# Cached attention and MLP over two layers: kept heads' scores in pairs, the first P.V of layer two ahead of the next scores, next queries under the maximum, last w4 rows apart

## The chip, the cores and the metric

One core of one Trainium2 chip. The metric is the device time of one execution in microseconds (us). A run of the kernel before and one of the kernel after are compared on the same chip; smaller is faster.

## What is computed

One token passes two layers, and each layer is an attention over a cached window and a small MLP. Both layers use the same weights and the same cache. Cut to what matters:

```python
# D = 640, 32 heads of Dh = 192, window W = 4096 of 32768 positions, F = 1536
def A(x):                                   # x: one row of 640
    q = (x @ wq).reshape(32, 192)
    s = einsum("hd,hkd->hk", q, k_cache[:, -4096:]) * 192 ** -0.5
    o = einsum("hk,hkd->hd", softmax(s), v_cache[:, -4096:])
    return o.reshape(6144) @ wo
def B(x):
    x1 = x + shifts(gelu(ln(x) @ w1)) @ w2  # the shifts move one row out: zero for S = 1
    return x1 + gelu(ln(x1) @ w3) @ w4
for _ in range(2):
    x = x + A(ln(x))
    x = x + B(ln(x))
```

With a sequence of one row every shifted part of the first MLP is zero, so w1 and w2 are never loaded. What remains to be loaded is 218 MB: for each layer 32 heads of keys and of values at 1536 KB each, wo, w3 and w4; wq once.

## The kernel before, in words

**Groups and slots.** The 32 heads form eight groups of four (`G`). One buffer ("slot") holds 128 x 6144 bf16, that is 12,288 bytes in each partition or 1536 KB: the keys of one head, its values, its transposed keys, or a fifth of wq. There are 15 slots; five hold wq for the whole run. A list `free` hands them out: `slot()` takes the one at the front, and a slot is put back at the end when the program has no further use of it. The order of `free` is fixed when the program is built, so the slot that a load will go to, and with it the instruction that the load waits for, is set by the order in which the program is written. One more buffer, `half` (128 x 3072), holds by turns the exponentials E and their transpose ET, the probabilities PT, the blocks of queries (`Q8_two`), and at the end of a layer the last rows of w4.

**Loads.** SyncE issues all loads in one queue, strictly in order. The list comes from `plan`: first the keys of the first group, then for each group its values alternating with the keys of the next group, and wo; at the end w3 and w4 (`load_w34`, L136 to L149). Each issue waits until the last reader of its slot is done, and for the load eight before it (eight semaphores are used in turn). `ahead` and `need` advance through the list.

**One head's scores.** The keys lie in HBM with positions along partitions; VectorE transposes them in 32 x 32 blocks in two halves (`trans_begin`, `trans_end`, L324; 1.75 us each) into a free slot. `kmm` (L350, products on L364) then multiplies a block of queries with the transposed keys: 12 products of 512 columns, whose outputs are 8 rows each. An output's first row chooses a column tile of TensorE's array: head 0 and 2 of a group use the tiles at rows 0 and 32, heads 1 and 3 those at rows 64 and 96. All products of a group go to one PSUM tile, `S_ps`.

**Queries.** `qproj` (L296) makes the queries of a group: 30 products with wq (`qT_ps`, L301), a spread by VectorE (`Xq`, L305), one product (`Qrep_ps`, L309), and a masked block by VectorE (L312). `qpair_a` and `qpair_b` (L272 to L294) do the same for two heads at a time.

**Softmax.** `soft_a` (L378) takes the maximum of each row (L380), transposes it on TensorE (L384) and takes the maximum again (L386). `soft_b` brings it back (L392) and takes the exponentials on ScalarE (L396). `soft_c` transposes them on VectorE (L402), moves them into place with 16 small products (L411) and copies the result to PT on ScalarE (L417); between these it ends the half transposed keys of the next group's first head.

**P.V.** `pv_rows` (L462, L471) multiplies a head's probabilities with its values: 16 products of 384 columns on four column tiles. For the last group of a layer the last two heads go through `pv_cols`.

**Order around the change.** Layer one runs the groups 0 to 7, layer two 7 to 0. Layer one leaves the transposed keys and the values of group 7 in eight slots, so layer two begins "warm": `attention` computes the scores of four kept heads at once with `kmm`, one head after the other, with the queries in two halves. Five loads are called for at this point (`need(G + 1)`): into the two slots of w3 and w4, and into the slots of the first three kept heads' transposed keys. Then follow softmax, the first half transpose of the next group's first head, that group's queries, and the rest of the softmax. In the main loop, for each head i, the next group's keys are transposed and multiplied first, and P.V of the current group's head i follows; behind i = 1 the queries of the group after next are made ahead of P.V.

**End of a layer.** `mixer` (L641) is the MLP: 60 products with w3 (L655), GELU, 60 with w4 (L666). The last 20 of these read four row blocks of w4 that one load of 640 KB brings into `half` (L147).

Of the kernel before, what the change touches and what calls it, by code (L numbers as in the profile page):

```python
# [8 lines left out]
BF16 = mybir.dt.bfloat16  # L9
# [15 lines left out]
def kernel(  # L25
# [110 lines left out]
    def load_w34():  # L136
# [11 lines left out]
            half[:, D - P:HALF].rearrange("p (k n) -> p k n", n=D),  # L148
            B_w4[(NB4 + 1) * P:NF * P, :].rearrange("(k p) n -> p k n", p=P))  # L149
# [122 lines left out]
    def qpair_a(g, x, xn_bf):  # L272
        qT_ps = psm.tile([P, NOC // 2], F32, tag="psm", name="qT_ps")
        for tl in range(NOC // 2):
            t = g * NOC + x * (NOC // 2) + tl
            for kc in range(ND):
                nc.tensor.matmul(
                    qT_ps[:, tl:tl + 1], lhsT=wq_t[kc][:, t * P:(t + 1) * P], rhs=xn_bf[:, kc:kc + 1],
                    start=(kc == 0), stop=(kc == ND - 1))
        Xq = sm.tile([P, NOC // 2, 4], BF16, name="Xq")  # L280
        nc.vector.tensor_tensor(
            out=Xq[:], in0=qT_ps[:, :].unsqueeze(2).broadcast_to([P, NOC // 2, 4]),
            in1=maskq[:, :].unsqueeze(1).broadcast_to([P, NOC // 2, 4]), op=ALU.mult)
        return Xq

    def qpair_b(g, x, Xq):
        Qrep_ps = psm.tile([P, 2 * NCOL], F32, tag="psm", name="Qrep_ps")
        nc.tensor.matmul(Qrep_ps[:], lhsT=Lb[:].rearrange("p a i -> p (a i)"), rhs=Xq[:].rearrange("p t b -> p (t b)"), start=True, stop=True)
        if x == 0:
            Q_t[g] = Q8_two[nq[0] % 2]  # L290
            nq[0] += 1
        nc.vector.tensor_tensor(
            out=Q_t[g][:, x], in0=Qrep_ps[:, :].unsqueeze(2).broadcast_to([P, 2 * NCOL, 8]),
            in1=blk8[:, x, :].unsqueeze(1).broadcast_to([P, 2 * NCOL, 8]), op=ALU.mult)  # L294

    def qproj(g, xn_bf):  # L296
        qT_ps = psm.tile([P, NOC], F32, tag="psm", name="qT_ps")
        for tl in range(NOC):
            t = g * NOC + tl
            for kc in range(ND):  # L300
                nc.tensor.matmul(  # L301
                    qT_ps[:, tl:tl + 1], lhsT=wq_t[kc][:, t * P:(t + 1) * P], rhs=xn_bf[:, kc:kc + 1],
                    start=(kc == 0), stop=(kc == ND - 1))
        Xq = sm.tile([P, NOC, 4], BF16, name="Xq")
        nc.vector.tensor_tensor(  # L305
            out=Xq[:], in0=qT_ps[:, :].unsqueeze(2).broadcast_to([P, NOC, 4]),
            in1=maskq[:, :].unsqueeze(1).broadcast_to([P, NOC, 4]), op=ALU.mult)
        Qrep_ps = psm.tile([P, NOC * 4], F32, tag="psm", name="Qrep_ps")
        nc.tensor.matmul(Qrep_ps[:], lhsT=Lb[:].rearrange("p a i -> p (a i)"), rhs=Xq[:].rearrange("p t b -> p (t b)"), start=True, stop=True)  # L309
        Q8 = Q8_two[nq[0] % 2]  # L310
        nq[0] += 1
        nc.vector.tensor_tensor(  # L312
            out=Q8,
            in0=Qrep_ps[:, :].rearrange("p (x c) -> p x c", x=2).unsqueeze(3).broadcast_to([P, 2, 2 * NCOL, 8]),
            in1=blk8[:].unsqueeze(2).broadcast_to([P, 2, 2 * NCOL, 8]), op=ALU.mult)
        Q_t[g] = Q8

# [32 lines left out]
    def kmm(g, i):  # L350
        h = g * G + i
        if i == 0:
            S_t[g] = S_two[nS[0] % 2]
            nS[0] += 1
        S_ps = S_t[g]
        T = T_t[h]
        x, par = i // 2, i % 2
        n = 0
        for f in range(NFB):
            for t in range(2):  # L360
                for hf in range(2):
                    Tv = T[:, hf * HALF:(hf + 1) * HALF].rearrange("p (f c t) -> p f c t", f=NFB, t=2)
                    r = 32 * (2 * par + hf)
                    nc.tensor.matmul(  # L364
                        S_ps[r:r + 8, :], lhsT=Q_t[g][:, x, par * NCOL + 2 * f + t, :], rhs=Tv[:, f, :, t],
                        start=(x == 0 and n == 0), stop=(n == NCOL - 1), tile_position=(0, r),
                        skip_group_check=True)
                n += 1
        if h not in keep_T:
            free.append(T_t.pop(h))  # L370
# [7 lines left out]
    def soft_a(g):  # L378
# [5 lines left out]
        nc.tensor.transpose(pmT_ps[0:G, :], pmh[:, 0:G], ident[:, :])  # L384
        ngm = sm.tile([G, 1], F32, name="ngm")
# [156 lines left out]
    def attention(order, xT_cur, xT_new, keep, loads):  # L542
# [30 lines left out]
        if warm:  # L573
            qpair_b(g0, 0, qpair_a(g0, 0, xn_bf))
            kmm(g0, 0)
            Xq = qpair_a(g0, 1, xn_bf)
            kmm(g0, 1)
            qpair_b(g0, 1, Xq)
            kmm(g0, 2)
            kmm(g0, 3)  # L580
            need(G + 1)
        else:
            qproj(g0, xn_bf)
            for i in range(G):
                keys(g0 * G + i)
                kmm(g0, i)
                if i == 0:
                    qproj(g1, xn_bf)
        soft_a(g0)
        soft_b(g0)  # L590
        if warm:
            keys(g1 * G, whole=False)
            qproj(g1, xn_bf)
        soft_c(g0, g1 * G)
        kept = lambda g, i: ("V", g * G + i) in keep
        for n, g in enumerate(order[:-1]):
            nxt = order[n + 1]
            ahead_h = order[n + 2] * G if n + 2 < len(order) else None
            for i in range(G):
                keys(nxt * G + i)  # L600
                kmm(nxt, i)
# [5 lines left out]
                ahead("V", g * G + i)  # L607
# [131 lines left out]
```

## Time and profile before

| What | Value |
|---|---|
| Median of three runs | 535.39 us (534.71 to 535.95) |
| Profiled execution: its own time | 535.32 us |
| Its span, first to last instruction | 533.5 us |
| TensorE, matmul busy | 314.8 us, 59% |
| VectorE busy | 279.2 us, 52% |
| ScalarE busy | 39.2 us, 7% |
| Moved by DMA | 218.76 MB, mean 410 GB/s |
| Mean granted TensorE clock | 0.678 of full speed |

The page gives for each engine its busy time, then the span in 40 slices of 13.3 us with the busy share in tenths, then the DMA queues. q1 is the queue of SyncE's loads; q8 and q14 fetch instructions. "Granted clock" is the share of TensorE's full clock in a stretch; in this trace it is 0.5 or 1.0 at any moment. In timelines a row gives start, duration, engine, line, operation, output and inputs, partitions and elements, and how many instructions were merged into the row; in brackets stands the idle time before it and what ended it. "SPq" is an issue on SyncE's queue. In the table of stretches the columns are the stretch, its length, busy time of PE (TensorE), PEld (its weight loads), DVE (VectorE), ACT (ScalarE) and POOL, then clock, DMA share and GB/s.

### The profile page before, as it was taken

What the parts mean: (1) busy time and instruction counts of PE and PEld (TensorE: products, weight loads), DVE (VectorE), ACT (ScalarE), POOL (GpSimd) and SP (SyncE); (2) the same over time, 40 slices, a digit from 0 to 9 for tenths busy, and PEclk for the clock granted to TensorE, in tenths of its full rate; (3) what the DMA queues carried; (4) which work ended last, traced back from release to release, by engine and by line L of the source; (5) the groups of instructions that cost most, each with busy time, mean ns of one, the idle gap of its engine ahead of it and who ended that gap; (6) DMA issues with size and microseconds to landing.
All of it is one profiled execution on the core that took longest, in us unless ns stands there. A gap on an engine that the chain in (4) does not pass through costs nothing.

```text
span 533.5 us, 8123 instructions
## 1 busy us (share of the span) xinstructions
PE 314.8 (59%) x3598; PEld 149.1 (28%) x3598; DVE 279.2 (52%) x409; ACT 39.2 (7%) x106; POOL 2.1 (0%) x11
## 2 busy tenths in 40 slices
PE   1154756574655656545585776765655657455685
PEld 0011222231322313213155333332322314122154
DVE  4076675465645457264421377775736447454421
ACT  1001010010100001010013001010101001010012
POOL 1000000000000000000000000000000000000000
PEclk9987677766577665776665777768577655756555
DMA  8999999999999999999999889999999999999995
GB/s 346 427 427 424 424 425 426 427 423 426 423 425 427 422 424 424 426 424 425 422 405 354 343 332 430 425 422 423 424 427 425 424 427 421 426 427 421 421 407 198
DMA packets 26151, 218.76 MB, mean 410 GB/s; under 512 B 2692, under 2 KB 7300, under 8 KB 10116
## 3 DMA queue, kind: packets, MB, share of 16 engines
q1 hardware_dynamic: 26106, 218.25, 98.1%
q8 instruction: 28, 0.46, 0.3%
q14 instruction: 7, 0.06, 0.0%
q10 hardware_dynamic: 10, 0.00, 0.0%
HBM read 218.24 MB, written 0.00 MB: 409 GB/s over the span
## 4 chain that ended last, share of the span: by engine, by line
DMA 75%; DVE 10%; PE 10%; SPq 4%; issue 1%; ACT 0%; DVEq 0%
DMA slot<-in_A_k_cache_dram 41%; DMA slot<-in_A_v_cache_dram 31%; DVE slot L324 7%; PE S_ps L364 6%; DMA half<-in_B_w_dram 3%; SPq L145 2%; DVE pm L380 1%; SPq L146 1%; PE O_ps L471 1%; PE qT_ps L301 0%; SPq L109 0%; DVE half L402 0%; PE pmT_ps L384 0%; PE y2T_ps L666 0%; DVE pmh L382 0%
## 5 line engine op out<-in xcount | busy, mean ns | idle before, releaser
L324 DVE STREAM_TRANSPOSE slot<-slot 128x1536 uint32<-128x1536 uint32 x120 | 206.8, 1756 | 84.0 <-DMA slot<-in_A_k_cache_dram 84.0
L364 PE MATMUL S_ps<-slot,half 128*8 128x512 bf16 x768 | 173.8, 558 | 113.9 <-DVE slot L324 112.1
L364 PEld LDWEIGHTS <-half 128*8 128x8 bf16 x768 | 45.5, 103 | 204.9 <-issue 193.9
L471 PE MATMUL O_ps<-slot,half 128*8 128x384 bf16 x512 | 61.7, 445 | 0.0
L471 PE MATMUL O_ps<-slot,PT 128*8 128x384 bf16 x448 | 47.0, 430 | 0.0
L394 ACT COPY nb_sb<-nb_ps 128x1 f32<-128x1 f32 x16 | 2.5, 159 | 425.2 <-PE nb_ps L392 425.2
L380 DVE TENSOR_REDUCE pm<-S_ps 128x1 f32<-128x512 f32 x16 | 11.1, 692 | 38.7 <-PE S_ps L364 38.7
L305 DVE TENSOR_TENSOR Xq<-qT_ps,maskq 128x24 bf16<-128x24 f32 x15 | 2.7, 179 | 50.3 <-PE qT_ps L301 50.3
L471 PEld LDWEIGHTS <-half 128*8 128x8 bf16 x512 | 19.7, 98 | 19.0 <-issue 16.3
L510 PE MATMUL OX_ps<-half,hoX 128*128 128x192 f32 x26 | 13.1, 608 | 15.6 <-DVE half L504 15.6
L301 PE MATMUL qT_ps<-xn_bf,slot 128*128 128x1 bf16 x450 | 14.2, 164 | 12.7 <-DMA slot<-in_A_wq_dram 11.5
L535 PE MATMUL y_ps<-osb,wo_g 128*128 128x1 bf16 x480 | 15.4, 165 | 10.5 <-DVE osb L516 9.2
L535 PEld LDWEIGHTS <-wo_g 128*128 128x128 bf16 x480 | 16.0, 105 | 16.0 <-issue 15.3
L471 PEld LDWEIGHTS <-PT 128*8 128x8 bf16 x448 | 15.3, 99 | 17.3 <-issue 14.7
L301 PEld LDWEIGHTS <-slot 128*128 128x128 bf16 x450 | 12.8, 97 | 19.8 <-DMA slot<-in_A_wq_dram 13.1
L384 PE MATMUL pmT_ps<-ident,pmh 128*4 128x128 f32 x16 | 5.0, 314 | 18.1 <-DVE pmh L382 18.1
L411 PE MATMUL Pp_ps<-half,identb 128*32 128x32 bf16 x256 | 6.6, 235 | 15.2 <-DVE half L402 15.2
L402 DVE STREAM_TRANSPOSE half<-half 128x512 bf16<-128x512 bf16 x16 | 11.0, 685 | 4.8 <-ACT half L396 4.8
L512 DVE TENSOR_TENSOR half<-OX_ps,m 128x192 f32<-128x192 f32 x13 | 4.7, 358 | 14.3 <-PE OX_ps L510 14.3
L411 PEld LDWEIGHTS <-identb 128*32 128x32 bf16 x256 | 5.8, 115 | 21.5 <-issue 21.1
L510 PEld LDWEIGHTS OX_ps<-half,hoX 128*128 128x128 f32 x26 | 6.5, 312 | 16.7 <-DVE half L504 16.7
L396 ACT ACTIVATE half<-S_ps,nb_sb 128x512 bf16<-128x512 f32 x16 | 11.0, 688 | 0.5
(116 smaller groups left out, 169.5 us busy)
## 6 DMA issues: line engine op xcount, KB each, us to landing
slot<-in_A_k_cache_dram SPq DMA_DIRECT2D x60, 1536.0 KB, 28.1
slot<-in_A_v_cache_dram SPq DMA_DIRECT2D x60, 1536.0 KB, 28.1
wo_g<-in_A_wo_dram SPq DMA_DIRECT2D x14, 960.0 KB, 28.1
slot<-in_A_wq_dram SPq DMA_DIRECT2D x5, 1536.0 KB, 13.2
slot<-in_B_w_dram SPq DMA_DIRECT2D x2, 1536.0 KB, 23.8
slot<-in_B_w_dram SPq DMA_DIRECT2D x2, 1120.0 KB, 19.4
half<-in_B_w_dram SPq DMA_DIRECT2D x2, 640.0 KB, 8.4
slot<-in_B_w_dram SPq DMA_DIRECT2D x2, 384.0 KB, 17.8
```

Source lines behind the costliest of these rows:

```text
L145: nc.sync.dma_start(b[:, FB4:FREE], B_w4[NB4 * P:(NB4 + 1) * P, 0:FREE - FB4])
L146: nc.sync.dma_start(half[:, 0:D - P], B_w4[NB4 * P:(NB4 + 1) * P, P:D])
L301: nc.tensor.matmul(qT_ps[:, tl:tl + 1], lhsT=wq_t[kc][:, t * P:(t + 1) * P], rhs=xn_bf[:, kc:kc + 1], start=(kc == 0), stop=(kc == ND - 1))
L324: nc.vector.transpose(T[:, hf * HALF:(hf + 1) * HALF].bitcast(U32).rearrange("p (f j k) -> p j f k", f=NFB, j=HJ, k=32), Kn[:, hf * HALF:( ...
L364: nc.tensor.matmul(S_ps[r:r + 8, :], lhsT=Q_t[g][:, x, par * NCOL + 2 * f + t, :], rhs=Tv[:, f, :, t], start=(x == 0 and n == 0), stop=(n ...
L380: nc.vector.tensor_reduce(out=pm[:], in_=S_t[g][:], op=ALU.max, axis=AX.X)
L396: nc.scalar.activation(out=E, in_=S_ps[:], func=ACTF.Exp, bias=nb_sb[:, 0:1], scale=scale, accum_out=lpart[:, 0:1])
L402: nc.vector.transpose(ET.rearrange("p (j r) -> p j r", r=32), E.rearrange("p (j k) -> p j k", k=32))
L411: nc.tensor.matmul(two, lhsT=identb[:, 32 * tl:32 * (tl + 1)], rhs=ETv[:, :, 0:2, m].rearrange("p (j e) x -> p x j e", e=2), start=True, s ...
L471: nc.tensor.matmul(O_t[g][r:r + 8, :], lhsT=PT[:, i, jj, :], rhs=V[:, jj * 2 * Dh:(jj + 1) * 2 * Dh], start=(i == 0 and jj < 4), stop=(i = ...
L510: nc.tensor.matmul(OX_ps[:], lhsT=hoX[:].rearrange("p h i -> p (h i)"), rhs=O_sb, start=True, stop=True)
L535: nc.tensor.matmul(y_ps[:, n:n + 1], lhsT=wo_t[g][:, 3 * pr + t, n * P:(n + 1) * P], rhs=osb[:, pr, t:t + 1], start=(first and t == chunks ...
```

## The change

Four edits. (1) The load of the last four row blocks of w4 becomes two: three row blocks, then one. (2) `kmm` takes a list of heads of a pair and interleaves their products; the four kept heads run as two pairs over four column tiles, and the second half of the queries is projected ahead of the first pair. In all other places `kmm` gets one head, as before. (3) The query functions are cut anew into `q_project` (products with wq), `q_spread` (Xq and Qrep) and `q_block`; at the start of layer two the next group's 30 products come ahead of the softmax, and `soft_a` calls `q_spread` behind the transpose of the maximum (`between`); the first half transpose of keys comes after the block of queries and `soft_b`. (4) In the first turn of the main loop of layer two, P.V of head i comes ahead of the next group's transposes and scores of head i. In all other turns the new `values(i)` is called where P.V stood, but the queries of the group after next, at i = 1, now follow it.

```diff
@@ load_w34
-            half[:, D - P:HALF].rearrange("p (k n) -> p k n", n=D),
-            B_w4[(NB4 + 1) * P:NF * P, :].rearrange("(k p) n -> p k n", p=P))
+            half[:, D - P:HALF - D].rearrange("p (k n) -> p k n", n=D),
+            B_w4[(NB4 + 1) * P:(NF - 1) * P, :].rearrange("(k p) n -> p k n", p=P))
+        nc.sync.dma_start(half[:, HALF - D:HALF], B_w4[(NF - 1) * P:NF * P, :])
@@ queries (qpair_a, qpair_b and the body of qproj become)
+    def q_project(g, xn_bf, xs=(0, 1)):
+        n = NOC // 2 * len(xs)
+        qT_ps = psm.tile([P, n], F32, tag="psm", name="qT_ps")
+        for tl in range(n):
+            t = g * NOC + xs[0] * (NOC // 2) + tl
             for kc in range(ND):
                 nc.tensor.matmul(
...
+        return qT_ps
+
+    def q_spread(qT_ps):
+        n = qT_ps.shape[1]
+        Xq = sm.tile([P, n, 4], BF16, name="Xq")
...
+        return Qrep_ps
+
+    def q_block(g, Qrep_ps, xs=(0, 1)):
+        if xs[0] == 0:
             Q_t[g] = Q8_two[nq[0] % 2]
             nq[0] += 1
...
     def qproj(g, xn_bf):
+        q_block(g, q_spread(q_project(g, xn_bf)))
@@ scores
-    def kmm(g, i):
-        h = g * G + i
-        if i == 0:
+    def kmm(g, x, pars):
+        if x == 0 and 0 in pars:
...
         for f in range(NFB):
             for t in range(2):
-                for hf in range(2):
...
+                for par in pars:
+                    T = T_t[g * G + 2 * x + par]
+                    for hf in range(2):
+                        Tv = T[:, hf * HALF:(hf + 1) * HALF].rearrange("p (f c t) -> p f c t", f=NFB, t=2)
+                        r = 32 * (2 * par + hf)
+                        nc.tensor.matmul(
+                            S_ps[r:r + 8, :], lhsT=Q_t[g][:, x, par * NCOL + 2 * f + t, :], rhs=Tv[:, f, :, t],
...
-    def soft_a(g):
+    def soft_a(g, between=None):
...
         nc.tensor.transpose(pmT_ps[0:G, :], pmh[:, 0:G], ident[:, :])
+        if between is not None:
+            between()
@@ attention, start of layer two
         if warm:
-            qpair_b(g0, 0, qpair_a(g0, 0, xn_bf))
-            kmm(g0, 0)
-            Xq = qpair_a(g0, 1, xn_bf)
-            kmm(g0, 1)
-            qpair_b(g0, 1, Xq)
-            kmm(g0, 2)
-            kmm(g0, 3)
+            Qrep_ps = q_spread(q_project(g0, xn_bf, (0,)))
+            q_block(g0, Qrep_ps, (0,))
+            qT_ps = q_project(g0, xn_bf, (1,))
+            kmm(g0, 0, (0, 1))
+            q_block(g0, q_spread(qT_ps), (1,))
+            kmm(g0, 1, (0, 1))
             need(G + 1)
+            qT_ps = q_project(g1, xn_bf)
+            got = []
+            soft_a(g0, lambda: got.append(q_spread(qT_ps)))
+            q_block(g1, got[0])
+            soft_b(g0)
+            keys(g1 * G, whole=False)
...
-        soft_a(g0)
-        soft_b(g0)
-        if warm:
-            keys(g1 * G, whole=False)
-            qproj(g1, xn_bf)
...
         soft_c(g0, g1 * G)
@@ attention, main loop
+            def values(i):
+                ahead("V", g * G + i)
+                if i == 0:
+                    norm_rows(g)
+                pv_rows(g, i, kept(g, i))
+
             for i in range(G):
+                first_v = warm and n == 0
+                if first_v:
+                    values(i)
                 keys(nxt * G + i)
-                kmm(nxt, i)
+                kmm(nxt, i // 2, (i % 2,))
...
-                ahead("V", g * G + i)
+                if not first_v:
+                    values(i)
                 if i == 1 and ahead_h is not None:
                     qproj(order[n + 2], xn_bf)
-                if i == 0:
-                    norm_rows(g)
-                pv_rows(g, i, kept(g, i))
```

## The prediction, made before the change was run

> **What bounds the kernel now.** I read the page's part 2 first (one column of the line is 13.3 us), then its part 3.
>
> ```profile
> DMA  8999999999999999999999889999999999999995
> GB/s 346 427 427 424 424 425 426 427 423 426 423 425 427 422 424 424 426 424 425 422 405 354 343 332 430 425 422 423 424 427 425 424 427 421 426 427 421 421 407 198
> q1 hardware_dynamic: 26106, 218.25, 98.1%
> q8 instruction: 28, 0.46, 0.3%
> ```
>
> The 16 DMA engines move 421 to 430 GB/s nearly always; the compute engines are 59% busy or less. The loads set the time, and only places where the DMA engines run dry can be won: the first column, the last, and four columns around 267 to 320 us, where layer one ends and layer two begins. Next, busy time by stretches of that region:
>
> ```profile
> 296.50:297.50 1.00, 1.00 (x6) 0.13 (x3) 0.00 (x0) 0.00 (x0) 0.00 (x0) 0.50 0.21 86
> 297.50:298.50 1.00, 1.00 (x21) 0.69 (x21) 0.17 (x1) 0.00 (x0) 0.00 (x0) 0.50 0.06 25
> 298.50:299.50 1.00, 1.00 (x12) 0.27 (x8) 0.00 (x0) 0.00 (x0) 0.00 (x0) 0.90 0.72 135
> ...
> 310.00:311.00 1.00, 1.00 (x14) 0.32 (x12) 1.00 (x1) 0.00 (x0) 0.00 (x0) 0.50 0.27 111
> 311.00:312.00 1.00, 1.00 (x16) 0.54 (x12) 1.00 (x2) 0.00 (x0) 0.00 (x0) 0.50 0.06 25
> 312.00:313.00 1.00, 0.75 (x8) 0.21 (x4) 0.86 (x1) 0.00 (x0) 0.00 (x0) 0.83 0.60 111
> 313.00:314.00 1.00, 1.00 (x10) 0.36 (x9) 0.00 (x0) 0.00 (x0) 0.00 (x0) 1.00 0.55 184
> ```
>
> The last two columns are DMA share and GB/s. Against 430 GB/s the first hole lacks 0.80 + 0.94 + 0.69 us and 0.14 in the next us: **2.6 us**. The second lacks 0.74 + 0.94 + 0.74 + 0.57: **3.0 us**. What they wait for is in SyncE's timeline (the issues):
>
> ```profile
> 289.51 0.33 SPq L116 DMA_DIRECT2D slot<-in_A_k_cache_dram  x1
> 297.61 0.33 SPq L116 DMA_DIRECT2D slot<-in_A_k_cache_dram  x1
> 299.85 0.33 SPq L116 DMA_DIRECT2D slot<-in_A_k_cache_dram  x1
> 301.83 0.33 SPq L116 DMA_DIRECT2D slot<-in_A_k_cache_dram  x1
> 311.61 0.33 SPq L116 DMA_DIRECT2D slot<-in_A_v_cache_dram  x1
> 312.72 0.33 SPq L116 DMA_DIRECT2D slot<-in_A_k_cache_dram  x1
> ```
>
> A 1536 KB load takes 3.69 us of DMA. The load of 289.51 is through at about 296.6. The next needs the slot of a kept head's keys, free when that head's scores end at 297.57. Three such loads last until 310.3; the one after them waits for head 0 of the next group (scores end 311.5). First bytes follow an issue by 0.96 us (297.61 to 298.57, 311.61 to 312.57 in the trace's packets).
>
> Last, the end of the chain of waits:
>
> ```profile
> 521.11 8.61 DMA half<-in_B_w_dram
> 529.71 0.05 issue
> 529.76 0.71 PE y2T_ps L666 x20
> 530.49 0.17 DVE x L670
> ```
>
> All 20 last w4 products wait for one 640 KB transfer.
>
> **Part 1: last w4 rows apart (both layers).** Products of one column follow each other by 27 ns (36 in 0.95 us from 288.36). Now 15 of the 20 need only the first three row blocks, so 15 x 0.027 = 0.40 us can run before the last bytes. On the slowest DMA engine the last block is 8 packets of 1280 bytes, 52 ns apart: 0.41 us, just enough to cover them. One more issue on SyncE costs 0.38 us. In layer one the load behind it is not issued until 287.53, 4.9 us later; at the end only the output is behind it, 10 us later. One more semaphore write per engine is 0.009 us. **-0.4 us at the end**, and queries 0.4 us earlier in layer two. Were the two transfers to land together, 0; bounds -0.45 to 0.1.
>
> **Part 2: scores two heads at a time.** The kept heads' scores today and a P.V that uses four column tiles:
>
> ```profile
> 294.85 2.72 PE L364 MATMUL S_ps<-slot,half 128*8 128x512 bf16 x12 [0.35 <-DVE half L292]
> 300.28 1.98 PE L364 MATMUL S_ps<-slot,half 128*8 128x512 bf16 x24 [0.35 <-DVE half L292]
> ```
> ```profile
> 272.00 2.73 PE L471 MATMUL O_ps<-slot,PT 128*8 128x384 bf16 x32
> ```
>
> Head 0: 12 products in 2.72 us at clock 0.5, six steps of two, 0.427 us apart. Heads 2 and 3: 24 in 1.98 us at clock 1.0; where both heads' products are in flight, four start within 20 ns and the next four 0.225 us later. P.V: 32 products in eight steps of four, 0.32 us apart, at clock 0.5. So four tiles step as fast as two, and a pair costs 5 x 0.427 + 0.63 = 2.76 us at clock 0.5 and 5 x 0.225 + 0.39 = 1.5 us at 1.0. The second query projection (15 products, 0.45 us) moves ahead of the pair, but TensorE is idle there from 294.5 to 294.85 for the block of queries: +0.05 us at most. Start 294.85 - 0.40 = 294.45; pair 0 ends at 297.2 (head 0 today: 297.57), Qrep and the block of queries take 0.46 us as today (299.82 to 300.28), pair 1 ends at 299.2 to 300.4, today 302.26. The first hole closes 0.4 us earlier (late DMA engine: 0.1, its last packet ends at 298.45): **-0.3 us**. Its rest stays: nothing frees a slot earlier.
>
> [...] The score row's next weight load starts at 295.24, together with the products of 295.24 and in the 0.63 us of those begun at 294.85, and the steps are 0.427 us, the 512 columns alone. [...]
>
> **Part 3: next queries under the maximum.** Today VectorE does maximum, half a transpose (1.75 us), then Xq, wait for Qrep, block of queries (305.62 to 306.40), then the exponentials' transpose. Now the 30 products (0.90 us) run under the maximum (0.69 + 0.23), Xq and Qrep beside the transpose on TensorE; 0.36 us of VectorE stays ahead of the half transpose. P is ready 5.65 us after the last score instead of 5.86: -0.2 us of a chain that Part 4 takes off the path.
>
> **Part 4: first P.V ahead of the next scores.** P is ready at 299.2..300.4 + 5.65; 16 products take 0.82 us (row at 326.42, clock 1.0) to 1.45 us (four steps of 0.32 and the tail, clock 0.5); V's slot is free at 305.7 to 307.5 and the next load is issued then, not at 311.61. Its first bytes come at 306.7 to 308.5; the loads in flight last until 310.35 - 0.40 = 309.95. So the second hole is gone, with 1.4 to 3.2 us to spare. What is late next: the load behind it in SyncE's order waits for scores of head 0, now behind that P.V: half transpose until 6.4 us after the last score, 2.0 to 3.1 us of scores, so 308.7 to 309.9, needed by 309.95 + 3.69 - 0.96 = 312.7. Then P.V 1, scores 1 (about 312.5, needed by 320) keep ahead. Each us of lateness costs one.
>
> What is the hole worth? For the mean DMA engine 3.0 us. One engine's last packet ends at 312.10 (the next latest 311.18, half by 310.6): a 16 KB instruction packet sat in its row at 307.88 for 1.02 us and doubled the next one to 0.93. It loses only 0.47 us plus 0.6 us of slow first packets, 1.1 us. The end belongs to the latest engine. Bounds 1.1 and 3.0; I take **-2.5 us**, nearer the row of the 16, since one engine had the short gap and the last loads land up to 3.5 us apart anyway.
>
> **Part 5: moved on the way.** From layer one on, the query projection of the group after next follows P.V 1 instead of preceding it. Behind Xq on VectorE queue the transposes of head 2, whose scores free a slot for SyncE. After V 1 lands: P.V 1.45, products 0.9, Xq to queries 0.9, together 3.25 us; head 2's keys land 3.69 us after V 1. Even 1 us late is covered: a load lands 28.1 us after its issue, seven loads deep. **0**; without that cover 1 us in each of 11 groups.
>
> **Sum.** 535.32 (profiled; span 533.5 and 1.8 around it; median of the three runs 535.39) - 0.4 - 0.3 - 2.5 = **532.1 us**.
>
> **Rivals.**
> 1. *Only the late engine counts* (instruction packets pile on one engine): -1.1 - 0.1 - 0.4 gives 533.7. For it: the spread of landings of 3.5 us at the end. Against: at 317.8 us the landings of one load lay within 0.7 us again, and the hits wander. Chance 0.14.
> 2. *The hole stays*, because the first load is freed by P.V but the loads behind it wait on VectorE (two transposes, 3.43 us, per head), and SyncE's queue is in order: only parts 1 and 2 count, 534.6; with noise, no change. Against: the margins above. Chance 0.07.
> 3. *Weight loads lie bare*: 24 x 0.084 us (the load's duration in the score rows) = 2.0 us more for pair 0, so the first hole grows by 1.6 us; second closed: 535.3 + 1.6 - 2.5 - 0.4 = 534.0. Against: steps of 0.427 us. Chance 0.04.
> 4. *Slower: the four tiles run in turn.* Place: pair 0, whose end frees both slots at once. At clock 0.5 24 x 0.427 = 10.2 us, slots free at 304.8, the first hole grows by 7 us; with 3 won elsewhere about 539. It decides from pair 0 over 6.1 us (2.76 + 0.4 + 2.5 + 0.4). For it: no score row at clock 0.5 has four tiles. Against: the four-tile rows above. Chance 0.05.
>
> Forecast 0.70, 531.1 to 533.3 (bounds of its terms, and the runs' scatter of 0.6 us).
>
> **Chances and range.** 0.2% is 1.1 us, about what a measurement of this kernel can tell from none. Faster: 0.70 + 0.13 + 0.02 = 0.85; same: 0.09; slower: 0.06. The range 531.1 to 534.4 takes in the forecast, rivals 1 and 3 and leaves out most of 2 and 4.
>
> **What would show it.** Scores of a pair: 24 products in about 2.8 us; first V load issued by 307.5; DMA share about 1.0 from 300 to 325; a hole of some 2.2 us left around 297; five products after the last transfer. I am wrong if a hole stands after 310, if pair 0 takes over 3.5 us, or if the holes are gone and the last landing is not over 2 us earlier.

## The result, and the profile after

| | before | after |
|---|---|---|
| Median of 6 runs each, same chip | 535.43 us (534.71 to 536.19) | **531.52 us** (531.15 to 532.27) |
| Profiled execution, its span | 535.32, 533.5 | 531.52, 529.7 |
| Ratio after / before | | 0.9928, 95% interval 0.9915 to 0.9941 |

Faster by 3.9 us, 0.7%. Forecast were 532.1 us and 531.1 to 534.4.

The page's parts 2 and 3 of after: the DMA share and the GB/s in 40 slices of 13.2 us, and two of the queues.

```profile
DMA  8999999999999999999999899999999999999996
GB/s 344 430 424 421 427 426 422 428 424 424 426 423 427 423 422 426 427 425 422 426 407 337 365 429 429 423 424 424 423 425 424 424 424 426 426 425 422 423 406 213
q1 hardware_dynamic: 26138, 218.25, 98.7%
q8 instruction: 28, 0.46, 0.3%
```

Of the three low slices behind the 407 (354, 343, 332 before) two are left, 337 and 365; the third is at 429. Bytes and instruction packets are the same as before. The same seven stretches of 1 us as in the prediction, of after (clock, DMA share and GB/s are the last three columns):

```profile
296.50:297.50 1.00, 0.78 (x9) 0.10 (x1) 0.18 (x1) 0.00 (x0) 0.00 (x0) 0.53 0.50 209
297.50:298.50 1.00, 0.87 (x16) 0.39 (x20) 0.08 (x1) 0.00 (x0) 0.00 (x0) 1.00 0.60 123
298.50:299.50 1.00, 1.00 (x28) 0.50 (x21) 0.26 (x1) 0.00 (x0) 0.00 (x0) 1.00 0.60 209
310.00:311.00 1.00, 1.00 (x14) 0.36 (x11) 0.00 (x0) 0.00 (x0) 0.00 (x0) 1.00 0.92 393
311.00:312.00 1.00, 0.73 (x30) 0.66 (x27) 0.18 (x1) 0.00 (x0) 0.00 (x0) 1.00 1.06 455
312.00:313.00 1.00, 0.92 (x17) 0.39 (x17) 0.80 (x2) 0.00 (x0) 0.00 (x0) 1.00 0.98 418
313.00:314.00 1.00, 0.00 (x0) 0.00 (x0) 1.00 (x1) 0.00 (x0) 0.00 (x0) 1.00 1.04 442
```

The second hole (310 to 314) is gone: 393 to 455 GB/s where 25 to 184 stood. The first (296.5 to 299.5) is narrower and not gone: 1.7 us are lost in these three stretches, 2.4 before. SyncE's issues of after in that region:

```profile
287.83 11.69 SPq L116 DMA_DIRECT2D slot<-in_A_k_cache_dram  x5
306.12 0.33 SPq L116 DMA_DIRECT2D slot<-in_A_v_cache_dram  x1
308.28 0.33 SPq L116 DMA_DIRECT2D slot<-in_A_k_cache_dram  x1
308.95 0.33 SPq L116 DMA_DIRECT2D slot<-in_A_v_cache_dram  x1
```

The first row merges the five loads called for at the warm start; the first load behind them is issued at 306.12, before at 311.61. The kept heads' scores of after on TensorE, two pairs instead of four heads:

```profile
294.43 2.73 PE L352 MATMUL S_ps<-slot,half 128*8 128x512 bf16 x24
297.63 1.53 PE L352 MATMUL S_ps<-slot,half 128*8 128x512 bf16 x24 [0.35 <-DVE half L299]
```

24 products on four tiles in 2.73 us at clock 0.5 and 1.53 at 1.0: forecast were 2.76 and 1.5. The last score ends at 299.2 (before 302.26). The end of the chain of waits:

```profile
517.50 8.29 DMA half<-in_B_w_dram
525.78 0.05 issue
525.83 0.70 PE y2T_ps L668 x20
526.54 0.02 issue
526.56 0.17 DVE x L672
```

The chain now passes through the three-row transfer, which lands at 525.78; the last row lands at 526.18, and the products end 0.35 us behind that (before: 529.71, and 0.76 us).

### The profile page after: what moved, and what is told of

Same layout as the page of the kernel before. It is cut to its first block, busy times and chain, and to the rows that moved or that the text cites. A ratio compares the mean times of both kernels' runs of the same rounds, so it can differ in the third digit from the quotient of the medians.

```text
span 529.7 us, 8126 instructions
## 1 busy us (share of the span) xinstructions
PE 310.7 (59%) x3598; PEld 151.5 (29%) x3598; DVE 279.4 (53%) x409; ACT 39.2 (7%) x106; POOL 2.1 (0%) x11
## 4 chain that ended last, share of the span: by engine, by line
DMA 69%; PE 13%; DVE 12%; SPq 3%; issue 1%; ACT 0%; DVEq 0%
DMA slot<-in_A_k_cache_dram 35%; DMA slot<-in_A_v_cache_dram 32%; DVE slot L313 9%; PE S_ps L352 8%; DMA half<-in_B_w_dram 3%; SPq L145 2%; PE O_ps L463 2%; PE qT_ps L279 1%; DVE pm L370 1%; SPq L109 0%; DVE half L394 0%; SPq L146 0%; PE y_ps L527 0%; PE pmT_ps L374 0%; PE y2T_ps L668 0%
## 5 line engine op out<-in xcount | busy, mean ns | idle before, releaser
L352 PE MATMUL S_ps<-slot,half 128*8 128x512 bf16 x768 | 168.8, 553 | 116.4 <-DVE slot L313 115.0
L463 PE MATMUL O_ps<-slot,half 128*8 128x384 bf16 x512 | 63.1, 432 | 0.4 <-ACT half L409 0.4
L463 PE MATMUL O_ps<-slot,PT 128*8 128x384 bf16 x448 | 56.7, 469 | 0.3 <-DMA slot<-in_A_v_cache_dram 0.3
L287 DVE TENSOR_TENSOR Xq<-qT_ps,maskq 128x24 bf16<-128x24 f32 (+1 forms) x17 | 3.1, 181 | 59.0 <-PE qT_ps L279 58.9
L279 PE MATMUL qT_ps<-xn_bf,slot 128*128 128x1 bf16 x480 | 15.4, 164 | 13.9 <-DMA slot<-in_A_wq_dram 11.5
L463 PEld LDWEIGHTS <-PT 128*8 128x8 bf16 x448 | 18.3, 102 | 17.4 <-issue 14.7
L279 PEld LDWEIGHTS <-slot 128*128 128x128 bf16 x480 | 13.8, 98 | 19.8 <-DMA slot<-in_A_wq_dram 13.2
L384 PE MATMUL nb_ps<-ngm,hsT 4*128 4x1 f32 x32 | 7.9, 313 | 5.9 <-DVE ngm L378 5.9
```

The lines of the kernel that those rows point to most:

```text
L279: nc.tensor.matmul(qT_ps[:, tl:tl + 1], lhsT=wq_t[kc][:, t * P:(t + 1) * P], rhs=xn_bf[:, kc:kc + 1], start=(kc == 0), stop=(kc == ND - 1))
L352: nc.tensor.matmul(S_ps[r:r + 8, :], lhsT=Q_t[g][:, x, par * NCOL + 2 * f + t, :], rhs=Tv[:, f, :, t], start=(x == 0 and n == 0), stop=(n ...
L384: nc.tensor.matmul(nb_ps[:], lhsT=hsT[0:G, :], rhs=sx[g]["ngm"][0:G, :], start=True, stop=True)
L463: nc.tensor.matmul(O_t[g][r:r + 8, :], lhsT=PT[:, i, jj, :], rhs=V[:, jj * 2 * Dh:(jj + 1) * 2 * Dh], start=(i == 0 and jj < 4), stop=(i = ...
```

## The experiments

**Theory:** the time follows the bytes that the 16 engines together fail to move, so each hole counts with its whole width; and the second hole is closed as soon as the first load behind the five is issued about 1 us before the loads in flight end, by whichever edit. **Rivals:** P.V. ahead of the scores alone closes it; only the latest engine's idle time counts.

To test the first half I keep an account. Of each kernel's trace I read the GB/s of three stretches (284 to 291 us, the MLP; 291 to 305, the first hole; 305 to 322, the second) and take length x (1 - GB/s / 430) as DMA time lost. Before, the stretches of 7, 14 and 17 us have:

```profile
284.00:291.00 7.00, 4.05 (x122) 3.83 (x122) 1.11 (x5) 3.67 (x7) 0.00 (x0) 0.50 0.91 309
291.00:305.00 14.00, 9.75 (x115) 4.46 (x113) 3.92 (x13) 1.26 (x6) 0.00 (x0) 0.73 0.85 347
305.00:322.00 17.00, 11.88 (x137) 5.14 (x135) 13.90 (x18) 1.02 (x3) 0.00 (x0) 0.72 0.87 355
```

Lost: 1.97 + 2.70 + 2.97 = 7.64 us. After:

```profile
284.00:291.00 7.00, 4.25 (x122) 3.94 (x122) 1.36 (x9) 3.91 (x10) 0.00 (x0) 0.50 0.87 286
291.00:305.00 14.00, 8.67 (x142) 4.78 (x146) 6.84 (x17) 2.23 (x8) 0.00 (x0) 0.74 0.91 373
305.00:322.00 17.00, 13.39 (x143) 5.06 (x135) 11.64 (x14) 0.00 (x0) 0.00 (x0) 0.72 1.01 427
```

Lost: 2.34 + 1.86 + 0.12 = 4.32 us. "Account" in the table is the difference of such sums from 7.64, less 0.41 us (0.76 - 0.35, the products behind the last landing) where w4 is split. "Measured" is the difference of the medians on the same chip; the ratio is worked out from all runs, and differs from that of the medians by up to 0.0006 (e4).

| Kernel | GB/s in the three stretches | lost, us | account | measured | ratio (95%) |
|---|---|---|---|---|---|
| after | 286, 373, 427 | 4.32 | -3.73 | -3.91 | 0.9928 (0.9915 to 0.9941) |
| e1 after without P.V. first | 301, 365, 426 | 4.38 | -3.67 | -3.71 | 0.9933 (0.9921 to 0.9946) |
| e2 P.V. first alone | 300, 354, 406 | 5.54 | -2.10 | -2.04 | 0.9963 (0.9950 to 0.9975) |
| e3 w4 split alone | 316, 360, 355 | 7.11 | -0.94 | -0.63 | 0.9990 (0.9981 to 0.9998) |
| e4 after without pairs | 309, 361, 415 | 4.81 | -3.24 | -3.20 | 0.9934 (0.9920 to 0.9947) |
| e5 queries behind P.V. 1 alone | 315, 353, 355 | 7.35 | -0.29 | -0.02 | 1.0001 (0.9992 to 1.0010) |
| e6 five products to raise the clock | 334, 360, 420 | 4.24 | -3.81 | -3.59 | 0.9934 (0.9922 to 0.9947) |
| e7 pair 0 done twice | 332, 289, 429 | 6.23 | -1.82 | -1.29 | 0.9972 (0.9962 to 0.9982) |
| e8 pairs and w4 alone | 307, 360, 424 | 4.52 | -3.53 | -3.42 | 0.9942 (0.9928 to 0.9955) |
| e10 three values kept, not four | 397, 407, 423 | 1.57 | -2.79 | -1.34 | 0.9971 (0.9959 to 0.9982) |
| e12 queries and w4 alone | 300, 370, 379 | 6.09 | -1.96 | -2.40 | 0.9960 (0.9946 to 0.9974) |
| e13 w4 by twelve rows | 210, 374, 422 | 5.72 | - | -2.31 | 0.9959 (0.9945 to 0.9972) |
| e14 w4 by four rows | 301, 382, 423 | 3.94 | -4.11 | -4.88 | 0.9914 (0.9900 to 0.9927) |

(e10 moves one load more, 3.69 us, which is in its account. e13 and e14 also gain in the last layer's w4, which no stretch here holds, and e13 has another end: below.)

The stretches come from one execution, the profiled one, and "measured" from the medians. Against what the profiled executions themselves took less than the median of before, the account is off by over 0.5 us in four kernels (e14 aside, below): e6 (account -3.81, execution -3.08), e7 (-1.82, -1.29), e10 (-2.79, -1.60) and e12 (-1.96, -0.78). In three of the four the last DMA engine lands further behind the median one than the 2.01 us of before: 2.46, 2.73 and 3.44 us in e6, e10 and e12 (1.92 in after). Adding that growth brings these three within 0.5 us; e7, with 1.77, stays open by 0.8 us.

### Which edit closes the second hole

**e1: after, but P.V. where it stood.**

```diff
-                first_v = warm and n == 0
+                first_v = False
```

> The changed kernel with P.V of the kept heads back behind the next scores; everything else as changed. Theory A (P.V first closes the second hole): the load behind the five then waits again for the scores of the next group's first head, which end 6.4 us plus 2.0 to 3.1 us after the last kept score, so at about 307.6 to 308.8 since the last score now ends at 299.2 instead of 302.26; first bytes 1 us later, at 308.6 to 309.8, where the loads in flight last until about 310. So even A, worked out anew from the trace of the changed kernel, gives hardly any hole: 531.5 to 532. Theory B, the step as the prediction put it (pairs and queries under the maximum are worth only 0.3 us, the second hole falls to P.V first): the hole comes back, 534 to 534.5. A result near 531.6 says that the second hole was closed twice over.

535.38 to 531.67. SyncE's issues of e1:

```profile
287.66 11.73 SPq L116 DMA_DIRECT2D slot<-in_A_k_cache_dram  x5
307.93 0.33 SPq L116 DMA_DIRECT2D slot<-in_A_v_cache_dram  x1
```

Without P.V. first the next load is issued at 307.93 instead of 306.12, and still before the loads in flight end: 426 GB/s from 305 to 322. The edit to which the prediction gave the 2.5 us is worth 0.2 us here, less than the interval.

**e2: before, with P.V. first and nothing else.**

```diff
+                first_v = warm and n == 0
+                if first_v:
+                    if i == 0:
+                        norm_rows(g)
+                    pv_rows(g, i, kept(g, i))
...
-                if i == 0:
-                    norm_rows(g)
-                pv_rows(g, i, kept(g, i))
+                if not first_v:
+                    if i == 0:
+                        norm_rows(g)
+                    pv_rows(g, i, kept(g, i))
```

> The kernel before with only the kept heads' P.V ahead of the next scores. P is ready at 308.1, P.V 0 takes 0.8 to 1.45 us, the next load is issued at 309.0 to 309.6 instead of 311.61, first bytes at 310.0 to 310.6; the loads in flight last until 310.3. Theory M (a hole costs what the mean DMA engine loses): the second hole of 3.0 us shrinks to 0 to 0.5, so 535.4 - 2.5 to -3.0 = 532.4 to 532.9. Theory L (only the latest DMA engine counts, 1.1 us): 534.3.

535.38 to 533.34. Issues of e2:

```profile
287.80 14.08 SPq L116 DMA_DIRECT2D slot<-in_A_k_cache_dram  x5
309.41 0.33 SPq L116 DMA_DIRECT2D slot<-in_A_v_cache_dram  x1
```

309.41, 2.2 us earlier than before, closes two thirds of the hole: 0.95 us lost in place of 2.97. That is more than the 0 to 0.5 us expected, and 533.34 lies above the expected 532.4 to 532.9. Alone P.V. first is neither needed (e1) nor enough.

**e8: before, with the w4 split and the pairs** (second half of the queries ahead of them); next queries, P.V. and transposes where they stood.

```diff
+            Qrep_ps = q_spread(q_project(g0, xn_bf, (0,)))
+            q_block(g0, Qrep_ps, (0,))
+            qT_ps = q_project(g0, xn_bf, (1,))
+            kmm(g0, 0, (0, 1))
+            q_block(g0, q_spread(qT_ps), (1,))
+            kmm(g0, 1, (0, 1))
...
```

> The kernel before with the last w4 rows apart and the kept heads' scores in pairs; next queries and P.V stay where they were. The last kept score should end as in the run without P.V first (its slot's load was issued at 299.06 there, at 301.04 with the w4 edit alone), 2.0 us sooner. The load behind the five was issued at 310.81 with the w4 edit alone, so now at about 308.8, first bytes at 309.8, when the loads in flight end (310): theory C (each of the edits that brings the next scores or P.V forward by over 2 us closes the second hole by itself): 0.1 to 0.4 us of hole left, ratio 0.993 to 0.994. Rival (pairs need the early queries or P.V first to pay): hole of 2.9 us as with the w4 edit alone, ratio 0.998 to 0.999.

535.37 to 531.95. Issues of e8:

```profile
287.52 11.94 SPq L116 DMA_DIRECT2D slot<-in_A_k_cache_dram  x5
308.47 0.33 SPq L116 DMA_DIRECT2D slot<-in_A_v_cache_dram  x1
```

Scores that end 3 us earlier bring the issue to 308.47, and 0.24 us is lost. This closes the same hole once more; -3.42 and e2's -2.04 do not add to after's -3.91.

**e12: after without pairs and without P.V. first** (left: query edits, w4).

```diff
-            kmm(g0, 0, (0, 1))
+            kmm(g0, 0, (0,))
+            kmm(g0, 0, (1,))
...
-            kmm(g0, 1, (0, 1))
+            kmm(g0, 1, (0,))
+            kmm(g0, 1, (1,))
...
-                first_v = warm and n == 0
+                first_v = False
```

> The changed kernel with P.V back behind the next scores and the kept heads one after the other on two tiles: of the change only the w4 edit, the second half of the queries ahead of all four heads' scores, and the next queries under the maximum are left. The last score ends 1.0 us later than with pairs, so the load behind the five is issued at 307.93 (measured without P.V first) + 1.0 = 308.9, first bytes at 309.9. Theory C: 0.1 to 0.5 us of hole, ratio 0.993 to 0.995. Rival (pairs carry it): hole of 2 us or more, ratio 0.997 to 0.999.

535.37 to 532.97 (532.60 to 534.59; the profiled run is the longest, the other four took 532.60 to 533.12). Issues and scores of e12:

```profile
287.60 13.20 SPq L116 DMA_DIRECT2D slot<-in_A_k_cache_dram  x5
309.75 0.33 SPq L116 DMA_DIRECT2D slot<-in_A_v_cache_dram  x1
```
```profile
294.22 3.54 PE L352 MATMUL S_ps<-slot,half 128*8 128x512 bf16 x24
298.24 2.63 PE L352 MATMUL S_ps<-slot,half 128*8 128x512 bf16 x24 [0.35 <-DVE half L299]
```

A miss: I expected the hole nearly gone, and 2.02 us of it stand in this trace. The second pair ran mostly at clock 0.5 (2.63 us; in e4, with the same order, 1.98), so the issue came at 309.75. In this run the granted clock rose at 299.72, in e4's at 298.29. How much of the hole stands in the four shorter runs no trace shows. Over all kernels the loss from 305 to 322 goes with that issue: 305.59 to 307.97: 0.04 to 0.59 us; 308.47: 0.24; 309.41: 0.95; 309.75: 2.02; 310.81 (e3) to 311.61: 2.97. The edge lies near 308.5. That is about 1 us, the time to first bytes (0.96 in before), ahead of the end of the loads in flight (in before 298.57 + 3 x 3.69 = 309.6).

### The parts beside it

**e3: before with the w4 split alone** (the first hunk of the change).

> The kernel before with only the last w4 rows loaded apart, in both layers. 15 of 20 products, 0.40 us, leave the end; in layer two the queries come 0.40 us earlier, which ends the first hole that much sooner. Theory M: -0.4 at the end and -0.4 in the first hole (the second hole moves as a whole): 534.6. Theory L: the latest DMA engine had only 0.1 us to lose in the first hole: -0.5, so 534.9. Were both transfers to land together: 535.4.

535.38 to 534.75, 11 runs: -0.63 (by the interval -1.0 to -0.1). That lies between the two theories' 534.6 and 534.9 and does not tell them apart. The kept scores begin at 294.33 (294.85 before), and the second hole has its full 2.97 us.

**e4: after without pairs** (the first two hunks of e12).

> The changed kernel with the kept heads' scores one after the other again on two column tiles (order of the rest as changed). Head 0 ends as pair 0 did (297.2), so the third load is issued as early, the fourth 1.9 us later, the fifth 1.9 us later still: the first hole stays as in the changed kernel. The last score ends at about 301.7 instead of 299.2, P.V 0 at 308 to 308.5, first bytes of the next load by 309.5, before the loads in flight end at about 310: theory A (P.V first covers alone): 531.5 to 531.8. If pairs carry the gain: up to 534.

535.38 to 532.18, above the expected 531.5 to 531.8 (the runs go from 531.15 to 532.63). Scores of e4:

```profile
294.52 3.55 PE L352 MATMUL S_ps<-slot,half 128*8 128x512 bf16 x24
298.54 1.98 PE L352 MATMUL S_ps<-slot,half 128*8 128x512 bf16 x24 [0.35 <-DVE half L299]
```

Two heads written one after the other take 3.55 us, not 2 x 2.72: the second head's products, which go to other column tiles, start at 295.34 beside the third of the first head's six steps. Interleaving saves 0.82 us in the first pair and 0.45 in the second. Both slots of the first pair then come free almost together (their loads are issued at 297.19 and 297.56 in after, at 297.28 and 298.10 in e4), and the account says 0.49 us; the intervals of the two ratios overlap. Of the 3.1 us by which the last score of after ends earlier than before (299.16, 302.26), 1.4 are the pairs (e4: 300.52) and about 1.0 the query projection that no longer lies between the heads (e3: 301.47).

**e5: before with only the queries behind P.V. 1.**

```diff
-                if i == 1 and ahead_h is not None:
-                    qproj(order[n + 2], xn_bf)
...
+                if i == 1 and ahead_h is not None:
+                    qproj(order[n + 2], xn_bf)
```

> The kernel before with only the query projection of the group after next moved behind P.V of head 1 (it was ahead of it) in both layers. Theory A (seven loads in flight cover a wait of about 1 us on VectorE): no change, 535.1 to 535.7. Rival: the transposes behind Xq on VectorE's queue start 1 us later in each of 12 groups and the slots with them; if the loads felt it, up to 12 us slower, 547; if only at the start of layer two, where few loads are in flight, up to 1 us slower.

534.61 to 534.59, 11 runs, ratio 0.9992 to 1.0010: nothing.

**e6: after with five products of zero weights**, 512 columns each, between 286.8 and 292.3 us, whose output nobody reads, to raise the clock before pair 0 (called three times in the MLP of layer one, and two at once ahead of the queries).

```diff
+    def warm_up(n):
+        for _ in range(n):
+            nc.tensor.matmul(Pp_ps[:, :], lhsT=zero_w[:, :], rhs=wq_t[0][:, 0:512], start=True, stop=True,
+                             skip_group_check=True)
...
```

> The changed kernel with five extra products of 512 columns by a weight tile of zeros (into a PSUM tile that is written anew before it is read) in the MLP of layer one and at the start of layer two, where TensorE idles between 287.7 and 293 us. If the granted clock is 1.0 when the first pair of scores starts, the pair takes 1.5 us instead of 2.73, the two slots are free 1.2 us sooner and the first hole shrinks by as much: theory M (the mean DMA engine counts) 530.3; theory L (the latest engine, whose last packets of the load before end after the new ones begin) 531.5. If the clock stays at 0.5: 531.5, or up to 532 where the extra products delay the chain to the queries.

534.61 to 531.02, the ratio of after within its interval. In e6:

```profile
288.92 0.59 PE L650 MATMUL Pp_ps<-slot,zero_w 128*128 128x512 bf16 x1
...
291.23 1.01 PE L650 MATMUL Pp_ps<-slot,zero_w 128*128 128x512 bf16 x2
...
293.92 2.73 PE L352 MATMUL S_ps<-slot,half 128*8 128x512 bf16 x24
...
297.12 2.33 PE L352 MATMUL S_ps<-slot,half 128*8 128x512 bf16 x24 [0.35 <-DVE half L299]
```

(Three of the five are recorded as products; all five weight loads are there, 286.8 to 291.2.) Pair 0 still takes 2.73 us: clock 0.5. The idea gave nothing to test the first hole with.

### What a hole is worth

**e7: after with pair 0's products done twice** (the second pass writes the same scores).

```diff
...
-            kmm(g0, 0, (0, 1))
+            kmm(g0, 0, (0, 1), times=2)
```

> The changed kernel with the first pair of scores done twice (the second pass starts the sums anew, so the result is that of one pass). This prices a late slot: pair 0 takes 2.56 us more at clock 0.5, less if the clock rises within it (1.3 at 1.0), so both slots come free 1.3 to 2.6 us later. Theory M: the first hole grows by just that, the second stays closed (its cover moves along): 531.5 + 1.3 to 2.6 = 532.8 to 534.1, equal to the growth that the trace shows. Theory L: the latest DMA engine works until 299.34 on the load before, so it loses 1.1 us less than that: 531.7 to 533.0.

534.61 to 533.32, 9 runs: -1.29. Scores of e7, and its stretch with the first hole:

```profile
294.01 5.00 PE L353 MATMUL S_ps<-slot,half 128*8 128x512 bf16 x48
```
```profile
291.00:305.00 14.00, 9.70 (x140) 4.71 (x141) 4.89 (x13) 1.40 (x5) 0.00 (x0) 0.73 0.72 289
```

The first slot's load is issued at 299.05 instead of 297.19, 1.86 us later. From 291 to 305 4.59 us are lost (after: 1.86), and by the two ratios (0.9972 - 0.9928) the kernel pays 0.0044 x 535 = 2.35 us. With both intervals that is 1.5 to 3.2 us: a late slot costs about its whole lateness, so the mean of the engines counts. The late-engine theory, by which 1.1 us less than the lateness would be paid, so 0.8 us, falls. For the second hole e2 says the same: 2.02 us less hole, 2.04 us won.

**e10: after with three values kept over the layers instead of four**, so a slot is free early and nothing has to wait for pair 0, for one load more.

```diff
-            need(G + 1)
+            need(G + 2)
...
-    keep = {("V", gl * G + i) for i in range(G)}
+    keep = {("V", gl * G + i) for i in range(G - 1)}
```

> The changed kernel with the values of three instead of four heads kept over to layer two: the fourth head's slot is free when layer one's last P.V ends, about 282.2, so a load of keys can be issued at 282.7, ahead of the MLP's end, and two more behind it; one load of 1536 KB more in all. The DMA engines then have work until about 300, and the next slot is free at 297.2. Theory M: the trace of the changed kernel lacks 2.5 us of DMA between 284 and 291 and 1.95 us between 291 and 305; of the first some 0.8 us stays (packets of 1280 bytes are slower), the rest goes, 3.6 us won, 3.69 us for the extra load: 531.2 to 532. If holes cost less than their width (theory L): 533 to 534.

534.61 to 533.27: a miss, I had expected 531.2 to 532. Issues of e10:

```profile
287.16 10.11 SPq L116 DMA_DIRECT2D slot<-in_A_k_cache_dram  x3
297.32 0.43 SPq L116 DMA_DIRECT2D slot<-in_A_v_cache_dram  x1
```

The stretch from 284 to 305 is nearly full (397 and 407 GB/s), as meant: 4.20 us lost become 1.29. But the added load takes 3.69, and the account's -2.79 is 1.45 us too good. In e10's profiled run the last landing is 2.73 us behind the median engine's, in before's 2.01; that explains 0.7 of the 1.45. The rest stays open.

### Longer packets for w4

In w4's transfers each row of 640 is a packet of 1280 bytes, 0.058 us at the end of after (22 bytes per ns; 12,288 bytes take 0.466 over the whole run, 26 per ns; the first expectation below has 0.052 and 0.457, a little low). If a partition holds consecutive rows of w4, packets grow (to 9216 and 4864 bytes in e13); w3's columns must then be taken with a stride, so that each partition's GELU output fits its rows.

**e13: after with twelve rows a partition.**

```diff
+        w4 = B_w4.rearrange("(p k) n -> p (k n)", p=P)
+        nc.sync.dma_start(b[:, F:FREE], w4[:, 0:FREE - F])
+        nc.sync.dma_start(half[:, 0:HALF - D], w4[:, FREE - F:NF * D - D])
+        nc.sync.dma_start(half[:, HALF - D:HALF], w4[:, NF * D - D:NF * D])
...
+        rows = a[:, kc * F:(kc + 1) * F] if kc < NKA else b[:, 0:F]
+        return rows.rearrange("p (q c) -> p c q", c=NF)[:, fc, :]
```

> The kernel after, but w4 is loaded with 12 consecutive rows in each partition (packets of 9216, 4864 and 1280 bytes, in three transfers), in place of 1280-byte packets and of two short pieces of 256 and 1024 bytes; w3's columns are taken with a stride of 12, so that GELU's output fits these rows. The output is the same. In the trace of after a packet of 1280 bytes takes 0.052 us, 24.7 bytes per ns, and one of 12,288 bytes 0.457 us, 26.9 per ns. Theory 1 (the mean engine sets the end, and every byte rate counts): 96 packets of 1280 bytes per engine and layer cost 0.004 us each more than long ones, 0.4 us per layer, and the short pieces some 0.1: -0.8 to -1.0 us against after, ratio 0.991. Theory 2 (at the MLP of layer one the DMA engines idle anyway until the first kept slot comes free, so only the last layer's gain counts): -0.4 to -0.5 us, ratio 0.992. Rival (weight loads with a stride slow the 60 products with w3, 27 ns apart now): their rows tell; if each takes 60 ns, 2 us more in layer one's MLP, ahead of the kept scores, and nothing at the end, where the products with w3 lie beside the transfer of w4: ratio 0.996.

535.71 to 533.40, some 1.7 us slower than after by the ratios. The rival's ratio came out, though it had expected nothing at the end. First after's products with w3 in layer one, then e13's; "PEld" is their weight loads:

```profile
286.06 1.68 PEld L657 LDWEIGHTS <-slot 128*128 128x128 bf16 x60 [1.33 <-issue]
286.08 1.74 PE L657 MATMUL hT_ps<-xnn,slot 128*128 128x1 bf16 x60 [1.27 <-DVE nt L255]
```
```profile
285.90 3.56 PEld L653 LDWEIGHTS <-slot 128*128 128x128 bf16 x60 [1.32 <-issue]
285.94 3.61 PE L653 MATMUL hT_ps<-xnn,slot 128*128 128x1 bf16 x60 [1.27 <-DVE nt L251]
```

Weights whose columns lie 24 bytes apart load in 59 ns, adjacent ones in 28. In layer one w3's slot comes free 1.7 us later (issue at 289.52, not 287.83); at the end the long transfer lands at 526.56 and the last row at 526.96, but the chain of products ends at 528.32, where after's ends at 526.53. So the 60 slower products with w3 do cost time there too.

**e14: after with three runs of four rows** (NR is 4), w3's columns with a stride of 4.

```diff
+        w4 = B_w4.rearrange("(j p k) n -> p j (k n)", p=P, k=NR)
+        run = NR * D
+        cut = FREE - F - run
+        nc.sync.dma_start(b[:, F:F + run], w4[:, 0, :])
+        nc.sync.dma_start(b[:, F + run:FREE], w4[:, 1, 0:cut])
+        nc.sync.dma_start(half[:, 0:run - cut], w4[:, 1, cut:run])
+        nc.sync.dma_start(half[:, run - cut:HALF - D], w4[:, 2, 0:run - D])
+        nc.sync.dma_start(half[:, HALF - D:HALF], w4[:, 2, run - D:run])
...
+        t, o = (a, kc * F) if kc < NKA else (b, 0)
+        o += fc // NR * NR * P
+        return t[:, o:o + NR * P].rearrange("p (q c) -> p c q", c=NR)[:, fc % NR, :]
```

> The kernel after, but w4 is loaded in three runs of four consecutive rows a partition (packets of 5120, 4096, 1024, 3840 and 1280 bytes, in five transfers as in the kernel after), and w3's columns are taken with a stride of 4 (8 bytes) in place of 12 (24 bytes). The output is the same. By the packets of the run with twelve rows (9216 bytes 0.352 us, 4864 bytes 0.187, 1024 bytes 0.046, 1280 bytes 0.058 at the end of the span) an engine's share of w4 takes 8 x 0.61 us here and 8 x 0.70 in the kernel after, 0.7 us less per layer. Theory 1 (a load of weights slows only where neighbouring columns lie more than 8 bytes apart): 60 weight loads in about 1.7 us as after, the last bytes 0.3 to 0.7 us earlier in each layer, -0.5 to -1.2 us against after, ratio 0.9905 to 0.992. Theory 2 (any stride costs what a stride of 12 costs): 60 loads in 3.6 us, and the chain of products decides both MLPs: ratio 0.996. In between (each load some 40 ns, 2.4 us for 60): the products with w3 still end ahead of the last transfer at the end, and the gain in layer one is lost: ratio 0.992 to 0.993. [...]

535.17 to **530.29 us** (530.20 to 531.39), ratio 0.9914 (0.9900 to 0.9927). In e14:

```profile
285.24 2.07 PEld L659 LDWEIGHTS <-slot 128*128 128x128 bf16 x60 [1.33 <-issue]
285.27 2.13 PE L659 MATMUL hT_ps<-xnn,slot 128*128 128x1 bf16 x60 [1.27 <-DVE nt L257]
```

A stride of 8 bytes costs 34 ns a load, 0.4 us for 60. The last w4 row of layer one lands at 289.44 (after: 290.37) and pair 0 begins at 293.49 (294.43); the last landing of all is at 524.87 (526.18). It beats the kernel before clearly. Against after the profiled runs say -1.31 us and the ratios -0.75, with intervals that overlap, so that it beats after is likely but not shown.

## Why the prediction came out right, and where its steps were off

1. *What bounds the kernel* (loads, and three places where they run dry): right. The account of lost DMA time (-3.32) and the 0.41 us behind the last landing give -3.73 of the -3.91 us. The account stays within 0.5 us of the medians in ten of the twelve kernels it was made for. The others are e7 (0.53) and e10 (1.45). For e14 that holds only with the 0.7 us that the expectation worked out for the last layer's w4, which lies outside the stretches. Against single executions it is less exact, as said above: how far the last engine lags at the end is not in it.
2. *Part 1, -0.4 at the end and queries 0.4 earlier:* right. 0.41 at the end; kept scores 0.42 earlier in after, 0.52 in e3; -0.63 measured alone.
3. *Part 2, two heads step as fast as one:* right to 0.03 us a pair. The first-hole term of -0.3 was also about right: from 284 to 305 4.20 us are lost instead of 4.67. e3, with the w4 split alone, loses 4.14 there, so this gain is the w4 split's and not the pairs'.
4. *Part 4, -2.5 us:* **mis-sized.** Measured 2.97 - 0.12 = 2.85 us. The term was drawn toward the one engine with the short gap; e2 (this hole) and e7 (the first) show that the whole width counts.
5. *Part 4, to which edit it belongs:* **wrong.** The prediction gave the hole to P.V. first and wrote that the 0.2 us of part 3 belong to a chain that part 4 takes off the path. It held the numbers for the check that it left out. The issue of 311.61 waits for a chain behind the last score; with that score 3.06 us earlier it comes at 308.55 without P.V. first, in time for the prediction's own 309.95 less 0.96, and e1 and e8 show 307.93 and 308.47. The hole was closed twice over; after has it closed by over 2 us more than needed. The sum was right, since the hole counts once, and in that the number had luck: the step that carried 2.5 of its 3.2 us was not the one that was needed. The range of part 2 shows where P.V. first would be needed: had pair 1 run at clock 0.5 and ended at 300.4, the issue without P.V. first would come at about 309.3 (300.4 + 8.9, the distance in e1), past the edge of 308.5. This is an estimate; no run has that case.
6. *Margins of part 4:* V issued at 306.12 (forecast 305.7 to 307.5); the keys behind it at 308.28 (308.7 to 309.9).
7. *Part 5, 0:* right by e5.
8. *Rivals:* (1) the late engine as the price of a hole falls by e7 and e2. Lateness is real as scatter, and a single execution pays for it: the last landing is 2.01 us behind the median engine in before, 1.92 in after, 2.73 in e10, 3.44 in e12's longest run. (2) The hole stays: falls by after's trace. (3) and (4), bare weight loads or tiles in turn: fall by 24 products in 2.73 us at clock 0.5. That loads might lie bare was the author's guess, and after's trace does not show it: in this row all four tiles use all 128 rows, a load takes up to 0.128 us beside running products, and the steps stay at 0.427 us.

## What to carry to other kernels

Where loads set the time, price a stall by the bytes that the queues fail to move, all engines together, and count it once: before you credit an edit, ask whether the others have already moved the waiting issue over the edge. Edits with one hole in view do not add up, and each can be nearly free to leave out once the rest is in. When the stall is gone, look at short packets near it: longer ones are worth a try (e14), but a wide stride in what reads the data can cost more than they gain (e13).

## What the runs showed of the hardware

- **Weight loads with a stride.** 128 x 128 bf16 weights took 28 ns a load with adjacent columns (after), 34 at 8 bytes apart (e14) and 59 at 24 (e13): 60 loads in 1.68, 2.07 and 3.56 us. With w3 no other stride was run.
- **Products of different column tiles overlap even when written one head after the other:** 24 in 3.55 us (e4) against 2 x 2.72; interleaved 2.73.
- **The clock.** Five 512-column products spread over 4 us before the scores left pair 0 at 0.5 (e6). Pair 1, 0.5 us behind pair 0, ran at 1.0 in after, e1, e7 and e8 (1.52 to 1.55 us), mostly at 0.5 in e6, e10 and e13 (2.33, 2.43, 2.35), and between in e14 (1.93). The granted clock changes at 298.69, 305.52 and 312.35 in before, at 297.43, 304.26 and 307.67 in after (3.41 or 6.83 us apart in the trace's record of the clock), so at other times in each of the two. What raises it no run shows, and a plan should not count on 1.0 here.
- **Instruction fetches beside the loads.** The 28 packets of 16 KB of queue q8 take 0.96 to 1.12 us each in after, and in before the data packet that begins at the end of one (308.88) took 0.93 us instead of 0.46; by the author's estimate they are a likely source of the late landings above, though no run here took them away.
